# Converting 64-bit weights between the matmuls of eight experts: smaller pieces with two buffers, and an output layer that goes row block by row block

## The chip, the cores and the metric

The kernel runs on 1 core of a Trainium2 chip. The metric is the device time of one execution in microseconds; a version is given by the median of its runs.

## What is computed

Three layers follow each other. A recurrent attention (an mLSTM: 2 batches, 8 heads, 768 steps, head size 40) gives 1536 tokens of 320 numbers. A mixture of 8 experts sends each token to two of them. A last layer multiplies, applies a softmax-weighted unit and a normalisation, and multiplies again. Cut to what matters here:

```python
for e in range(E):                       # 8 experts, 320 -> 1024 -> 320
    for k in range(2):
        mask = top2[:, k] == e
        h = np.maximum(x[mask] @ w1[e], 0.0)
        out[mask] += top2_w[mask, k, None] * (h @ w2[e])
...
h = x @ w_in                             # the last layer
...
ln = (solu - mu) / np.sqrt(var + 1e-06) * g_ln
return ln @ w_out
```

The weights `moe2_w_in` and `moe2_w_out` of the last layer arrive as 64-bit floats. The kernel turns them into 32-bit floats on the chip, with integer operations on the two halves of each number.

## The kernel before

All matrix products are made from high and low parts: an operand is split into a part that TensorE multiplies as it is and the rest, and two or three products are added. So each weight is first split, on ScalarE (`split_hi`, line 117, a copy that rounds) and on VectorE or GpSimd (`split_lo`, line 121, the difference).

The expert stage is the loop over e at line 1019. The experts' row counts fall (`CAPS`: 448, 448, 432, 416, 404, 396, 384, 448); of expert 0 the first 192 rows are done before the loop. For each expert:

- The hidden layer, called L1 here. Eight groups f of 128 hidden columns: `layer1` (lines 127 to 134) makes 8 matmuls into an accumulator `ph`; `cut_h` then writes the hidden values, first the rounded part on ScalarE (line 139), then the rest on VectorE (line 140, and line 142 for the last 64 rows). The accumulators rotate: groups 0, 1, 3 to 7 share two, group 2 has one of another pool, so group 3 needs the accumulator of group 0. Between the groups stand three splits of the next expert's first weights (low parts on GpSimd, 128x1024 each), the transposes that prepare the next expert's rows (`prep_x`, line 988), and the load of the rows of the expert after that.
- The output layer, called L2 here. `layer2` (lines 149 to 154) makes, for one group f and one block n of 128 rows, 3 matmuls into the accumulator `pos[n]` (2 for a last short block of 64 rows). The loop is over f outside and n inside, so all row blocks end together. After each f stands one step of the conversion, and after every second f one split of the next expert's second weights (`split`, line 1025: ScalarE, VectorE, and a new load into the buffer that came free).
- `put(n)` (line 1055): the accumulator is copied to `YS`, on VectorE (line 164) except for n = 2, which goes on ScalarE; a short block is an addition on VectorE behind a copy on ScalarE (lines 161 and 162). GpSimd scatters the rows to DRAM (line 166).

The conversion (`convert`, line 928) takes a piece of raw weights `R` that SyncE has loaded, and makes one ScalarE instruction (line 937, a square that finds tiny numbers) and seven on VectorE (lines 938 to 942, 946, 947); the result in `u` is stored to DRAM (line 948), from where it is loaded as the weights of a ninth "expert". There are six pieces, five of 1024 columns and one of 512, in the order `cvs`: first `wout`, then `win`. The tiles `R`, `u`, `sc` and `sq` have one buffer each. The seven VectorE steps run through all experts as one sequence, one step after each f of experts 1 to 6; the next raw piece is loaded when the fifth instruction has read the old one.

```python
            act.activation(sq, hi.bitcast(F32), AF.Square)
            yield ve.tensor_scalar(u, hi, 3, (1 << 30) - 1, op0=ALU.logical_shift_left, op1=ALU.bitwise_and)
...
            sp.dma_start(dst[:, c0 : c0 + n], uf)
```

The order of instructions on each engine is that of the program text: no scheduler moves them, and an engine that waits holds everything behind it.

Expert 7 is written apart (line 1084): its L2 already goes row block by row block, and the tiles of the last layer's first steps take over the memory of the conversion's tiles by their tags.

Of the kernel before, what the change touches and what calls it, by code (L numbers as in the profile page):

```python
# [8 lines left out]
F32 = mybir.dt.float32  # L9
F32R = mybir.dt.float32r  # L10
BF16 = mybir.dt.bfloat16
I32 = mybir.dt.int32
# [8 lines left out]
DM, NE, DFF, NT = 320, 8, 1024, 1536  # L21
P = 128
# [14 lines left out]
def fused_kernel(ctx: ExitStack, tc, qt, kt, kv, og, ig, fg, wgn, noise, w1, w2, win, wout, gln, cst, out):  # L37
# [12 lines left out]
    wi32 = dp.tile([P, 3 * DFF], F32, name="wi32")  # L50
# [857 lines left out]
    with ExitStack() as pbx:  # L908
# [5 lines left out]
        psh = pbx.enter_context(tc.tile_pool(name="psh", bufs=2, space=PSUM))  # L914
        pso = pbx.enter_context(tc.tile_pool(name="pso", bufs=1, space=PSUM))

        cvs = (3, 4, 5, 0, 1, 2)
        raw = {}

        def load_raw(i):  # L920

            src = win if i < 3 else wout
            c0 = (i % 3) * DFF
            n = min(DFF, src.shape[1] - c0)
            R = raw[i] = b1.tile([P, DFF, 2], I32, tag="R", name=f"cvR{i}")[:, :n]
            sp.dma_start(R.rearrange("p n t -> p (n t)"), src[:, c0 : c0 + n].bitcast(I32))

        def convert(i):

            R, dst = raw[i], (wi32 if i < 3 else wo32)  # L930
            c0, n = (i % 3) * DFF, R.shape[1]
            u = b1.tile([P, DFF], I32, tag="u", name=f"cvu{i}")[:, :n]
            sc = b1.tile([P, DFF], I32, tag="sc", name=f"cvs{i}")[:, :n]
            sq = b1.tile([P, DFF], F32, tag="sq", name=f"cvq{i}")[:, :n]
            lo, hi = R[:, :, 0], R[:, :, 1]
            uf, scf = u.bitcast(F32), sc.bitcast(F32)
            act.activation(sq, hi.bitcast(F32), AF.Square)  # L937
            yield ve.tensor_scalar(u, hi, 3, (1 << 30) - 1, op0=ALU.logical_shift_left, op1=ALU.bitwise_and)
            yield ve.scalar_tensor_tensor(u, hi, -(1 << 30), u, op0=ALU.bitwise_and, op1=ALU.bitwise_or)
            yield ve.tensor_scalar(sc, u, -(1 << 23), None, op0=ALU.bitwise_and)  # L940
            yield ve.scalar_tensor_tensor(lo, lo, 9, sc, op0=ALU.logical_shift_right, op1=ALU.bitwise_or)
            ve.tensor_sub(scf, lo.bitcast(F32), scf)
            if i != cvs[-1]:
                load_raw(cvs[cvs.index(i) + 1])
            yield
            yield ve.scalar_tensor_tensor(uf, scf, 2.0**-20, uf, op0=ALU.mult, op1=ALU.add)
            ve.scalar_tensor_tensor(uf, sq, 2.0**-30, uf, op0=ALU.is_ge, op1=ALU.mult)
            sp.dma_start(dst[:, c0 : c0 + n], uf)
            yield

        X = {}
# [42 lines left out]
                act.activation(v["H"][0:64, d, 0:r], pt[0:64, 0:r], AF.Copy)  # L994
                ve.tensor_sub(v["H"][64:128, d, 0:r], pt[64:128, 0:r], v["T"][64:128, 0:r].bitcast(F32))

        def conversions():
            for i in cvs:
                yield from convert(i)

        X[0] = dict(x=rest, n=CAP - EARLY, w=[P] * ((CAP - EARLY) // P))
        load_x(1)

# [11 lines left out]
                    prep_x(0, d)  # L1015
        for n in range(2):
            put_y((0, n), YS[n], early["po"][n], T3, eti[:, n : n + 1], n == 1, ve)
        cv = conversions()
        for e in range(NE):
            n_e = X[e]["n"]  # L1020
            XH, XL = (X[e][k][:, :, 0:n_e] for k in "HL")
            new_w(e + 1, wsp1 if e % 2 == 0 else wsp0)
            hs = []

            def split(j):
                split_hi(e + 1, j)
                split_lo(e + 1, j, pool if j < 3 and e + 1 < NE else ve)
                if e + 2 < NE or e + 2 == NE and j != 2:
                    load_w(e + 2, j)

            for f in range(8):
                ph = (pst if f == 2 else psh).tile([P, CAP], F32, tag="pt" if f == 2 else "ph", name=f"ph{e}_{f}")[:, 0:n_e]
                layer1(ph, splits[e], XH, XL, f)
                h = bh.tile([P, 2 * CAP], F32R, tag="h", name=f"h{e}_{f}")
                cut_h(h, ph, n_e)
                hs.append(h)
                if e + 1 == NE and f % 2 == 0:
                    gain(NE, 3 + f // 2)
                if f % 2 and f < 7:
                    split(f // 2 + (3 if e + 1 == NE else 0))  # L1040
                if e == 0 and f == 7:
                    load_raw(cvs[0])
                if e + 1 < NE:
                    if f == 1:
                        alloc_x(e + 1)
                    if f in (2, 4, 6):
                        prep_x(e + 1, f // 2 - 1)
                    if f == 6 and e + 2 < NE:
                        load_x(e + 2)
            ws = X[e]["w"]  # L1050
            pos = [pos_tile(n, f"po{e}_{n}") for n in range(len(ws))]
            YS = [b1.tile([P, DM], F32, tag=f"YS{n}", name=f"YS{e}_{n}") for n in range(len(ws))]
            T3 = b1.tile([P, DM], F32, tag="T3", name=f"T3{e}")

            def put(n):
                put_y((e, n, 1), YS[n], pos[n], T3, X[e]["ti"][:, n : n + 1], ws[n] < P, act if n == 2 and e + 1 < NE else ve)

            if e + 1 < NE:
                for f in range(8):
                    for n in range(len(ws)):  # L1060
                        layer2(pos[n], splits[e], hs[f], f, n, n_e)
                    if e > 0:
                        next(cv, None)
                    if f % 2 == 0:
                        split(3 + f // 2)
                for n in range(len(ws)):
                    put(n)
                if e == NE - 2:
                    load_w(NE, 2)
            else:  # L1070
                tags = dict(Y="R", x2="u", XH="sc", XL="sq", T="T", pt="pt")
                held = {}

                def newb(t):
                    def new(k, shape, dt):
                        if k not in ("Y", "x2"):
                            return (pst if k == "pt" else b1).tile(shape, dt, tag=tags[k], name=f"c{k}{t}")
                        if k not in held:
                            held[k] = b1.tile([P, 3 if k == "Y" else 2] + shape[1:], dt, tag=tags[k], name=f"c{k}")
                        return held[k][:, t]  # L1080

                    return new

                for n in range(4):
                    for f in range(8):
                        layer2(pos[n], splits[e], hs[f], f, n, n_e)
                        if n == 0 and f == 0:
                            split(6)
                        if n == 1 and f < 3:
                            split(f)  # L1090
                        if n == 3 and f == 4:
                            xt(0, newb(0))
                            split_x(0, newb(0))
                    put(n)
                    if n < 3:
                        ahead.append((n, load_y(n, newb(n))))
                    if n == 2:
                        mix(0, newb(0))
                mix(1, newb(1))
# [202 lines left out]
```

## Time and profile before

| | us |
|---|---|
| median of 3 runs | 458.82 |
| lowest and highest run | 456.35, 461.11 |
| profiled execution, its time | 459.58 |
| its span in the trace | 457.5 |
| TensorE busy | 433.5 (95% of the span) |
| VectorE busy | 297.1 (65%) |
| ScalarE busy | 238.9 (52%) |
| GpSimd busy | 191.8 (42%) |

The span is the trace's own length; the execution takes 2.1 us more around it. Line numbers are those of the kernel before. PE is TensorE (PEld its weight loads), DVE is VectorE, ACT ScalarE, POOL GpSimd, SP SyncE; an engine's name with q is its queue.

### The profile page before, as it was taken

How to read it: one execution, taken by the hardware profiler on the slowest of the kernel's cores; microseconds unless marked ns; L12 is line 12 of the kernel's file. 1: busy time of each engine (PE TensorE's matmuls, PEld its weight loads, DVE VectorE, ACT ScalarE, POOL GpSimd, SP SyncE). 2: the span in 40 equal slices, each digit the busy share in tenths (PEclk: the TensorE clock that was granted, in tenths of full speed). 3: DMA queues.
4: the chain of work that ended last, by engine and by line, in shares of the span. 5: the costliest groups of instructions: out<-in, count | busy, mean ns of one | idle time of the engine just before them, and what ended most of it. 6: DMA issues, size and time to landing. Idle time of an engine off the chain costs nothing.

```text
span 457.5 us, 8125 instructions
## 1 busy us (share of the span) xinstructions
PE 433.5 (95%) x2777; PEld 407.1 (89%) x2777; DVE 297.1 (65%) x722; ACT 238.9 (52%) x517; POOL 191.8 (42%) x277
## 2 busy tenths in 40 slices
PE   7998979999989999999999969979999999999996
PEld 4887979998978989899999969969999789989996
DVE  8696698797446558575647665486355877556541
ACT  4687574661327362644626156236382776665542
POOL 8534666676317250541807218045203253342340
PEclk9999785896599999999999998989999999999999
DMA  6777894664424947375483834834602411120001
GB/s 187 245 225 219 295 273 133 229 239 148 179 85 143 323 135 271 125 239 181 129 302 91 319 113 137 295 101 127 211 1 102 147 45 43 45 85 16 29 16 43
DMA packets 36094, 71.73 MB, mean 157 GB/s; under 512 B 4225, under 2 KB 18981, under 8 KB 35408
## 3 DMA queue, kind: packets, MB, share of 16 engines
q1 hardware_dynamic: 32896, 62.06, 42.3%
q0 software_dynamic: 2912, 8.68, 5.2%
q8 instruction: 24, 0.39, 0.4%
q10 hardware_dynamic: 240, 0.41, 0.3%
q14 instruction: 22, 0.18, 0.1%
HBM read 55.50 MB, written 16.21 MB: 157 GB/s over the span
## 4 chain that ended last, share of the span: by engine, by line
PE 51%; DVE 9%; DMA 5%; issue 3%; ACT 1%; DVEq 0%; ACTq 0%
PE cpo L1173 3%; PE cpo L1175 3%; PE cpo L1174 3%; PE ph L127 3%; DMA wi<-cvu 3%; PE po L149 3%; PE po L150 3%; PE po L151 3%; PE pz L1165 2%; PE ph L128 2%; PE ph L133 2%; PE ph L130 2%; PE ph L132 2%; PE ph L129 2%; PE ph L131 2%
## 5 line engine op out<-in xcount | busy, mean ns | idle before, releaser
L166 POOL DMA_INDIRECT yt<-YS,ti x29 | 28.9, 995 | 126.4 <-DVE YS L164 119.8
L140 DVE SCALAR_TENSOR_TENSOR h<-ph,h 128x384 fp32r<-128x384 f32 (+1 forms) x64 | 34.3, 537 | 39.6 <-ACT h L139 39.5
L121 POOL TENSOR_TENSOR w0l<-r,w0h 128x1024 fp32r<-128x1024 f32 x23 | 54.7, 2408 | 9.8 <-ACT w0h L117 9.5
L139 ACT ACTIVATE h<-ph 128x448 fp32r<-128x448 f32 (+6 forms) x64 | 32.0, 503 | 48.1 <-PE ph L134 47.5
L149 PE MATMUL po<-w1h,h 128*128 128x320 f32 x184 | 56.8, 308 | 0.0
L151 PE MATMUL po<-w1h,h 128*128 128x320 f32 x184 | 56.7, 308 | 0.0
L150 PE MATMUL po<-w1l,h 128*128 128x320 f32 x184 | 56.7, 308 | 0.0
L476 POOL DMA_INDIRECT xg<-x,slots x24 | 25.8, 1075 | 27.6 <-DVE ix L444 12.5
L149 PEld LDWEIGHTS po<-w1h,h 128*128 128x128 f32 x184 | 34.6, 188 | 0.0
L150 PEld LDWEIGHTS po<-w1l,h 128*128 128x128 f32 x184 | 34.6, 188 | 0.0
L151 PEld LDWEIGHTS po<-w1h,h 128*128 128x128 f32 x184 | 34.6, 188 | 0.0
L340 PE MATMUL S<-Qb,Kb 128*128 128x128 f32 x192 | 32.9, 310 | 0.0
L127 PE MATMUL ph<-XH,w0h 128*128 128x448 f32 (+6 forms) x64 | 24.5, 383 | 7.9 <-DVE h L142 4.8
L121 DVE TENSOR_TENSOR w1l<-r,w1h 128x640 fp32r<-128x640 f32 x34 | 31.3, 934 | 0.4 <-ACT w1h L117 0.4
L937 ACT ACTIVATE cvq<-cvR 128x1024 f32<-128x1024 f32 (+1 forms) x6 | 6.3, 1052 | 46.0 <-DMA cvR<-in_win_dram 27.2
L1167 DVE TENSOR_TENSOR ZL<-pz,ZH 128x512 fp32r<-128x512 f32 x24 | 15.4, 685 | 22.6 <-ACT ZH L1166 22.6
L1173 PE MATMUL cpo<-w1h,ZH 128*128 128x320 f32 x96 | 30.0, 312 | 0.0
L1175 PE MATMUL cpo<-w1h,ZL 128*128 128x320 f32 x96 | 29.7, 309 | 0.0
L1174 PE MATMUL cpo<-w1l,ZH 128*128 128x320 f32 x96 | 29.7, 309 | 0.0
L117 ACT ACTIVATE w0h<-r 128x1024 fp32r<-128x1024 f32 x27 | 28.2, 1051 | 0.0
L340 PEld LDWEIGHTS S<-Qb,Kb 128*128 128x128 f32 x192 | 27.6, 214 | 0.1
L380 PE MATMUL Y<-KV,E 128*128 128x41 f32 x192 | 27.0, 296 | 0.0
(266 smaller groups left out, 1262.2 us busy)
## 6 DMA issues: line engine op xcount, KB each, us to landing
r<-in_w_dram SPq DMA_DIRECT2D x24, 512.0 KB
r<-in_w_dram SPq DMA_DIRECT2D x32, 320.0 KB
E<-gd SPq DMA_DIRECT2D x8, 512.0 KB
X<-xg SPq DMA_DIRECT2D x7, 579.0 KB
KV<-in_kv_dram SPq DMA_DIRECT2D x12, 324.0 KB
cY<-yt SPq DMA_DIRECT2D x12, 320.0 KB
cvR<-in_win_dram SPq DMA_DIRECT2D x3, 1024.0 KB
cvR<-in_wout_dram SPq DMA_DIRECT2D x2, 1024.0 KB
```

The costliest lines, as they stand in the source:

```text
L121: eng.tensor_sub(splits[e][2 * m + 1][:, k : k + n], raws[e, j], splits[e][2 * m][:, k : k + n].bitcast(F32))
L127: pe.matmul(ph, W1H[:, 0, fs], XH[:, 0], start=True, stop=False)
L139: act.activation(h[:, 0:n], ph, AF.Relu)
L140: ve.scalar_tensor_tensor(h[:, n + r : n + r + w], ph[:, 0:w], 0.0, h[:, 0:w].bitcast(F32), op0=ALU.max, op1=ALU.subtract)
L149: pe.matmul(po, hh, W2H[:, f], start=a, stop=False)
L150: pe.matmul(po, hh, W2L[:, f], start=False, stop=False)
L151: pe.matmul(po, hl, W2H[:, f], start=False, stop=z)
L166: i = pool.indirect_dma_start(out=yt, out_offset=bass.IndirectOffsetOnAxis(ap=idx[0:w], axis=0), in_=YS[0:w], in_offset=None, bounds_check ...
L340: pe.matmul(S[:, a], Kb[i % 3][j][:, a], Qb[i % 3][:, a], start=True, stop=True)
L1173: pe.matmul(po, ZH[:, f], W2H[:, f], start=(f == 0), stop=False)
L1174: pe.matmul(po, ZH[:, f], W2L[:, f], start=False, stop=False)
L1175: pe.matmul(po, ZL[:, f], W2H[:, f], start=False, stop=(f == 7))
```

## The change

A piece has 512 columns: five pieces of `wout` and six of `win`, eleven in all, in that order. `R`, `u` and `sq` have two buffers each, by the piece's parity; `sc` keeps one. Experts 1 to 5 convert two pieces each and expert 6 one; a piece's load is issued when the piece two before it has been read. The L2 of experts 0 to 6 goes row block by row block; a step is one group f of one block, a conversion step follows two of three steps, and the splits stand after steps 0, 6, 12 and 18 (0, 3, 6 and 9 in expert 0). `put(n)` follows its row block, and its copy is on ScalarE for every n except in expert 7. The tiles of the last layer's start take other tags.

```diff
-        cvs = (3, 4, 5, 0, 1, 2)
+        CW = 512
+        cvs = [(wo32, wout, c) for c in range(0, 8 * DM, CW)] + [(wi32, win, c) for c in range(0, 3 * DFF, CW)]
...
         def load_raw(i):
 
-            src = win if i < 3 else wout
-            c0 = (i % 3) * DFF
-            n = min(DFF, src.shape[1] - c0)
-            R = raw[i] = b1.tile([P, DFF, 2], I32, tag="R", name=f"cvR{i}")[:, :n]
-            sp.dma_start(R.rearrange("p n t -> p (n t)"), src[:, c0 : c0 + n].bitcast(I32))
+            if i < len(cvs):
+                _, src, c = cvs[i]
+                R = raw[i] = b1.tile([P, CW, 2], I32, tag=f"R{i % 2}", name=f"cvR{i}")
+                sp.dma_start(R.rearrange("p n t -> p (n t)"), src[:, c : c + CW].bitcast(I32))
...
-            u = b1.tile([P, DFF], I32, tag="u", name=f"cvu{i}")[:, :n]
-            sc = b1.tile([P, DFF], I32, tag="sc", name=f"cvs{i}")[:, :n]
-            sq = b1.tile([P, DFF], F32, tag="sq", name=f"cvq{i}")[:, :n]
+            R, (dst, _, c) = raw[i], cvs[i]
+            u = b1.tile([P, CW], I32, tag=f"u{i % 2}", name=f"cvu{i}")
+            sc = b1.tile([P, CW], I32, tag="sc", name=f"cvs{i}")
+            sq = b1.tile([P, CW], F32, tag=f"sq{i % 2}", name=f"cvq{i}")
...
-            if i != cvs[-1]:
-                load_raw(cvs[cvs.index(i) + 1])
+            load_raw(i + 2)
...
-            sp.dma_start(dst[:, c0 : c0 + n], uf)
+            sp.dma_start(dst[:, c : c + CW], uf)
...
                 if e == 0 and f == 7:
-                    load_raw(cvs[0])
+                    load_raw(0)
+                    load_raw(1)
...
-                put_y((e, n, 1), YS[n], pos[n], T3, X[e]["ti"][:, n : n + 1], ws[n] < P, act if n == 2 and e + 1 < NE else ve)
+                put_y((e, n, 1), YS[n], pos[n], T3, X[e]["ti"][:, n : n + 1], ws[n] < P, act if e + 1 < NE else ve)
 
             if e + 1 < NE:
-                for f in range(8):
-                    for n in range(len(ws)):
+                cv = chain(*(convert(i) for i in range(2 * e - 2, min(2 * e, len(cvs))) if e > 0))
+                for n in range(len(ws)):
+                    for f in range(8):
                         layer2(pos[n], splits[e], hs[f], f, n, n_e)
-                    if e > 0:
-                        next(cv, None)
-                    if f % 2 == 0:
-                        split(3 + f // 2)
-                for n in range(len(ws)):
+                        s = 8 * n + f
+                        if s % 3 < 2:
+                            next(cv, None)
+                        q = 6 if e > 0 else 3
+                        if s % q == 0 and s < 4 * q:
+                            split(3 + s // q)
                     put(n)
...
-                tags = dict(Y="R", x2="u", XH="sc", XL="sq", T="T", pt="pt")
...
+                tags = dict(Y=("R0", "R1", "Y2"), x2=("u0", "u1"), XH=("sq0",), XL=("sq1",), T=("T",), pt=("pt", "pt"))
```

VectorE at the end of the L2 of expert 4 and the start of the L1 of expert 5, before. `cv` marks the conversion's tiles with the piece's number (here pieces of `win`), `w1l_5` the low parts of expert 5's second weights, `YS4_n` the copies of expert 4's row blocks, `h5_0` the first hidden group of expert 5.

```order
L947 SCALAR_TENSOR_TENSOR cvu0_4191<-cvq0_4193,cvu0_4191 128x1024
L938 TENSOR_SCALAR cvu1_4475<-cvR1_4433 128x1024
L121 TENSOR_TENSOR w1l_5_4248<-r5_5_4178,w1h_5_4247 128x640
L939 SCALAR_TENSOR_TENSOR cvu1_4475<-cvR1_4433,cvu1_4475 128x1024
L940 TENSOR_SCALAR cvs1_4476<-cvu1_4475 128x1024
L121 TENSOR_TENSOR w1l_5_4248<-r5_6_4210,w1h_5_4247 128x640
L941 SCALAR_TENSOR_TENSOR cvR1_4433<-cvR1_4433,cvs1_4476 128x1024
L164 COPY YS4_0_4400<-po4_0_4396 128x320
L164 COPY YS4_1_4401<-po4_1_4397 128x320
L162 TENSOR_TENSOR YS4_3_4403<-po4_3_4399,T34_4404 64x320
L140 SCALAR_TENSOR_TENSOR h5_0_4558<-ph5_0_4549,h5_0_4558 128x384
```

The same place after the change; lines behind the conversion's first have moved by one to three.

```order
L945 SCALAR_TENSOR_TENSOR cvu6_4445<-cvq6_4447,cvu6_4445 128x512
L937 TENSOR_SCALAR cvu7_4502<-cvR7_4225 128x512
L938 SCALAR_TENSOR_TENSOR cvu7_4502<-cvR7_4225,cvu7_4502 128x512
L121 TENSOR_TENSOR w1l_5_4285<-r5_5_4203,w1h_5_4284 128x640
L939 TENSOR_SCALAR cvs7_4503<-cvu7_4502 128x512
L940 SCALAR_TENSOR_TENSOR cvR7_4225<-cvR7_4225,cvs7_4503 128x512
L941 TENSOR_TENSOR cvs7_4503<-cvR7_4225,cvs7_4503 128x512
L944 SCALAR_TENSOR_TENSOR cvu7_4502<-cvs7_4503,cvu7_4502 128x512
L121 TENSOR_TENSOR w1l_5_4285<-r5_6_4236,w1h_5_4284 128x640
L945 SCALAR_TENSOR_TENSOR cvu7_4502<-cvq7_4504,cvu7_4502 128x512
L162 TENSOR_TENSOR YS4_3_4440<-po4_3_4436,T34_4441 64x320
L140 SCALAR_TENSOR_TENSOR h5_0_4608<-ph5_0_4599,h5_0_4608 128x384
```

Before, a piece begins in the middle of the sequence and its tail stands behind the hidden groups of the next expert; now two whole pieces lie within one L2, piece 7 has another `u` than piece 6, and the two copies are gone from this engine.

ScalarE at the same place, from the last hidden group of expert 4 to the first of expert 5, before. `w1h_5` are the high parts of the weights, `cvq` the square.

```order
L139 ACTIVATE h4_7_4392<-ph4_7_4383 128x404
L117 ACTIVATE w1h_5_4247<-r5_3_4119 128x640
L117 ACTIVATE w1h_5_4247<-r5_4_4149 128x640
L937 ACTIVATE cvq1_4477<-cvR1_4433 128x1024
L117 ACTIVATE w1h_5_4247<-r5_5_4178 128x640
L117 ACTIVATE w1h_5_4247<-r5_6_4210 128x640
L164 ACTIVATE YS4_2_4402<-po4_2_4398 128x320
L161 ACTIVATE T34_4404<-po4_3_4399 64x320
L139 ACTIVATE h5_0_4558<-ph5_0_4549 128x396
```

The same after the change.

```order
L139 ACTIVATE h4_7_4429<-ph4_7_4420 128x404
L936 ACTIVATE cvq6_4447<-cvR6_4163 128x512
L117 ACTIVATE w1h_5_4284<-r5_3_4139 128x640
L117 ACTIVATE w1h_5_4284<-r5_4_4167 128x640
L164 ACTIVATE YS4_0_4437<-po4_0_4433 128x320
L936 ACTIVATE cvq7_4504<-cvR7_4225 128x512
L117 ACTIVATE w1h_5_4284<-r5_5_4203 128x640
L164 ACTIVATE YS4_1_4438<-po4_1_4434 128x320
L117 ACTIVATE w1h_5_4284<-r5_6_4236 128x640
L164 ACTIVATE YS4_2_4439<-po4_2_4435 128x320
L161 ACTIVATE T34_4441<-po4_3_4436 64x320
L139 ACTIVATE h5_0_4608<-ph5_0_4599 128x396
```

The copies of `YS` now stand between the squares and splits, each behind its row block, and there are two squares instead of one.

## Rows read from the trace of the kernel before

**Rows 1.** Waits, experts 1 to 6: engine, line, waited for; us, times, longest.

```profile
DVE cvu L938 <- DMA wo<-cvu: 14.7, 3, 6.1
DVE cvu L938 <- DMA wi<-cvu: 12.6, 2, 6.6
PE ph L127 <- DVE h L142: 4.8, 3, 3.9
PE ph L127 <- DVE h L140: 3.1, 1, 3.1
```

**Rows 2.** Stretches: length, busy PE PEld DVE ACT POOL, PEclk, DMA share, GB/s.

```profile
154.60:169.87 15.27, 15.27 (x79) 13.37 (x77) 7.33 (x22) 8.76 (x14) 9.05 (x6) 1.00 0.64 226
169.87:182.77 12.90, 12.90 (x89) 12.90 (x88) 11.01 (x14) 4.07 (x6) 0.18 (x2) 1.00 0.74 241
182.77:198.01 15.24, 14.75 (x78) 13.37 (x77) 8.23 (x24) 10.48 (x17) 9.92 (x10) 1.00 0.39 137
...
210.89:225.51 14.62, 14.23 (x78) 13.30 (x77) 9.18 (x26) 9.40 (x17) 9.61 (x10) 1.00 0.33 103
...
238.36:252.43 14.07, 13.99 (x78) 13.12 (x77) 10.62 (x27) 9.36 (x17) 9.42 (x10) 1.00 0.31 98
...
265.36:283.60 18.24, 14.35 (x76) 14.00 (x74) 11.92 (x26) 10.66 (x19) 10.11 (x10) 0.91 0.32 96
...
296.45:314.47 18.02, 14.93 (x79) 14.04 (x77) 12.57 (x22) 9.14 (x16) 10.43 (x10) 0.91 0.34 99
...
338.27:351.20 12.93, 12.93 (x90) 12.92 (x89) 6.89 (x11) 4.95 (x7) 3.92 (x6) 1.00 0.22 73
```

**Rows 3.** Two stretches within the L1 of expert 5.

```profile
270.20:274.06 3.86, 0.00 (x0) 0.03 (x1) 3.86 (x9) 0.62 (x2) 1.08 (x2) 1.00 0.46 128
274.06:277.50 3.44, 3.44 (x11) 3.43 (x12) 1.75 (x7) 0.64 (x2) 2.94 (x5) 0.55 0.40 144
```

**Rows 4.** VectorE in time: start, us, engine, line; in brackets idle before, releaser.

```profile
258.37 0.82 DVE L121 TENSOR_TENSOR w1l<-r,w1h 128x640 fp32r<-128x640 f32 x1
259.11 1.22 DVE L947 SCALAR_TENSOR_TENSOR cvu<-cvq,cvu 128x1024 f32<-128x1024 f32 x1
266.97 0.69 DVE L938 TENSOR_SCALAR cvu<-cvR 128x1024 int32<-128x1024 int32 x1 [6.64 <-DMA wi<-cvu]
...
273.24 0.54 DVE L140 SCALAR_TENSOR_TENSOR h<-ph,h 128x384 fp32r<-128x384 f32 x1
```

**Rows 5.** VectorE's groups by line and form: busy us, mean ns of one.

```profile
L164 DVE COPY YS<-po 128x320 f32<-128x320 f32 x17 | 7.7, 484 | 9.9 <-PE po L151 9.9
...
L942 DVE TENSOR_TENSOR cvs<-cvR,cvs 128x512 f32<-128x512 f32 x1 | 0.7, 693 | 0.0
...
L940 DVE TENSOR_SCALAR cvs<-cvu 128x512 int32<-128x512 int32 x1 | 0.5, 468 | 0.0
L938 DVE TENSOR_SCALAR cvu<-cvR 128x512 int32<-128x512 int32 x1 | 0.4, 427 | 4.6 <-DMA wo<-cvu 4.6
```

**Rows 6.** SyncE in time: the raw piece used in the L2 of expert 4.

```profile
257.22 0.34 SPq L926 DMA_DIRECT2D cvR<-in_win_dram  x1
```

**Rows 7.** ScalarE in time, end of expert 4's L2, and one group.

```profile
264.91 1.13 ACT L937 ACTIVATE cvq<-cvR 128x1024 f32<-128x1024 f32 x1 [10.46 <-DMA cvR<-in_win_dram]
265.94 1.35 ACT L117 ACTIVATE w1h<-r 128x640 fp32r<-128x640 f32 x2
...
L164 ACT ACTIVATE YS<-po 128x320 f32<-128x320 f32 x6 | 2.6, 429 | 7.6 <-issue 7.5
```

**Rows 8.** GpSimd and VectorE in time, experts 4 and 5.

```profile
251.79 2.44 POOL L121 TENSOR_TENSOR w0l<-r,w0h 128x1024 fp32r<-128x1024 f32 x1
253.84 1.49 DVE L941 SCALAR_TENSOR_TENSOR cvR<-cvR,cvs 128x1024 int32<-128x1024 int32 x1
...
274.11 0.97 POOL L166 DMA_INDIRECT yt<-YS,ti  x1 [0.22 <-DVE h L142]
```

**Rows 9.** VectorE: the cut of expert 5's eighth group, L2 from 283.60.

```profile
285.14 0.21 DVE L142 SCALAR_TENSOR_TENSOR h<-ph,h 128x64 fp32r<-128x64 f32 x1
```

More of the change, by code (lines that the diff above doesn't have):

```diff
@@ L915, in fused_kernel @@
         pso = pbx.enter_context(tc.tile_pool(name="pso", bufs=1, space=PSUM))
-        cvs = (3, 4, 5, 0, 1, 2)
+        CW = 512
+        cvs = [(wo32, wout, c) for c in range(0, 8 * DM, CW)] + [(wi32, win, c) for c in range(0, 3 * DFF, CW)]
         raw = {}
         def load_raw(i):
-            src = win if i < 3 else wout
-            c0 = (i % 3) * DFF
-            n = min(DFF, src.shape[1] - c0)
-            R = raw[i] = b1.tile([P, DFF, 2], I32, tag="R", name=f"cvR{i}")[:, :n]
-            sp.dma_start(R.rearrange("p n t -> p (n t)"), src[:, c0 : c0 + n].bitcast(I32))
-        def convert(i):
-            R, dst = raw[i], (wi32 if i < 3 else wo32)
-            c0, n = (i % 3) * DFF, R.shape[1]
-            u = b1.tile([P, DFF], I32, tag="u", name=f"cvu{i}")[:, :n]
-            sc = b1.tile([P, DFF], I32, tag="sc", name=f"cvs{i}")[:, :n]
-            sq = b1.tile([P, DFF], F32, tag="sq", name=f"cvq{i}")[:, :n]
+            if i < len(cvs):
+                _, src, c = cvs[i]
+                R = raw[i] = b1.tile([P, CW, 2], I32, tag=f"R{i % 2}", name=f"cvR{i}")
+                sp.dma_start(R.rearrange("p n t -> p (n t)"), src[:, c : c + CW].bitcast(I32))
+        def convert(i):
+            R, (dst, _, c) = raw[i], cvs[i]
+            u = b1.tile([P, CW], I32, tag=f"u{i % 2}", name=f"cvu{i}")
+            sc = b1.tile([P, CW], I32, tag="sc", name=f"cvs{i}")
+            sq = b1.tile([P, CW], F32, tag=f"sq{i % 2}", name=f"cvq{i}")
             lo, hi = R[:, :, 0], R[:, :, 1]
@@ L995, in prep_x @@
                 ve.tensor_sub(v["H"][64:128, d, 0:r], pt[64:128, 0:r], v["T"][64:128, 0:r].bitcast(F32))
-        def conversions():
-            for i in cvs:
-                yield from convert(i)
         X[0] = dict(x=rest, n=CAP - EARLY, w=[P] * ((CAP - EARLY) // P))
@@ L1017, in fused_kernel @@
             put_y((0, n), YS[n], early["po"][n], T3, eti[:, n : n + 1], n == 1, ve)
-        cv = conversions()
         for e in range(NE):
@@ L1070, in fused_kernel @@
             else:
-                tags = dict(Y="R", x2="u", XH="sc", XL="sq", T="T", pt="pt")
-                held = {}
+                tags = dict(Y=("R0", "R1", "Y2"), x2=("u0", "u1"), XH=("sq0",), XL=("sq1",), T=("T",), pt=("pt", "pt"))
                 def newb(t):
[L1075 to L1082, printed above, removed]
+                    return lambda k, shape, dt: (pst if k == "pt" else b1).tile(shape, dt, tag=tags[k][t], name=f"c{k}{t}")
                 for n in range(4):
```

## The prediction

> **What bounds the kernel now.** I read the idle times of TensorE first, then the stretch in which they lie, then the queue of the engine that ended them. In the list of waits for the experts' stretch [rows 1] the reader is to see that TensorE waits there for one thing only: the first matmul of a hidden-layer group (line 127) for a VectorE instruction of an earlier group (lines 140 and 142, the second half of `cut_h`), 4.8 + 3.1 us. The same list has a longer wait on another engine: VectorE stands 14.7 + 12.6 us at line 938, the first instruction of a conversion, for the store of the conversion before.
>
> The table of stretches [rows 2] gives the hidden layer (L1) and the output layer (L2) of each expert. An L2 takes 12.9 us whoever is late. The L1s are uneven: 15.27 us for expert 1 with 448 rows and 14.07 for expert 4 with 404 are full to within 0.1 us, so a row costs (15.27 - 14.07)/44 = 0.0273 us. By that line expert 2 (432 rows) should take 14.83, expert 3 (416) 14.40, expert 5 (396) 13.85 and expert 6 (384) 13.52; they take 15.24, 14.62, 18.24 and 18.02. The excess is 0.41 + 0.22 + 4.39 + 4.50 = 9.52 us, more than the 7.9 us of idle time. The rest is clock: in expert 5 TensorE stands still for 3.86 us, and the 3.44 us behind that are granted 0.55 of full speed on the mean, mostly the lower of its two levels, 1.2 of 2.4 GHz [rows 3].
>
> VectorE's queue says why [rows 4]. The last instruction of one conversion ends at 260.33 us and the next conversion, first in line behind it, has one buffer `u` with it; it starts at 266.97, when the store has landed, 6.64 us later. Behind it in the queue stand three conversion instructions, two weight splits, two copies of `YS` and one addition; only at 273.24 comes the cut of the first hidden group of expert 5, whose L1 began at 265.36 [rows 2]. TensorE needs that group's accumulator for its fourth group at 270.2. So a DMA round trip, through VectorE's order, stops TensorE. ScalarE is held in the same way: the load of a raw piece is issued at 257.22 [rows 6], in the middle of the L2 that uses it, and line 937 begins at 264.91 after 10.46 us [rows 7], with two splits and the copies behind it.
>
> **The change part by part.** *Two buffers.* Pieces alternate between `R0`/`R1`, `u0`/`u1`, `sq0`/`sq1`, and piece i uses what piece i - 2 used, one expert earlier. A store then has one expert's L1 plus L2 (27 us) to land instead of none; the one shown took about 6.6 [rows 4]. A load is issued when piece i - 2 is half done, some 20 us before its use; the one shown took 264.91 - 257.22 = 7.7 us [rows 6, 7]. Halved transfers need not take half: between nothing saved (7.7 and 6.6) and half, both ends are far below 20, so I put both waits at zero. This takes all of the 9.52 us, if VectorE isn't late for another reason.
>
> *Smaller pieces, more instructions.* A 1024-column piece costs VectorE 5 x 1.22 + 2 x 0.69 = 7.5 us [rows 4]; a 512-column piece 0.43 and 0.47 plus, at 0.69 for each of the five with two inputs, 3.45: 4.35 us [rows 5]. Eleven pieces are 47.9 us where five whole ones and a half took 41.9: 6.0 us more. Against it 14 copies of `YS`, of 0.48 us each [rows 5], go from VectorE to ScalarE: 6.8 us less. For VectorE the two cancel.
>
> *Does VectorE finish inside an L2?* In experts 1 to 5 there are two pieces, 8.7 us, and four splits of 0.82 [rows 4], 3.28. The cut of the eighth group ends 1.75 us after the L2 of expert 5 began (285.14 + 0.21 - 283.60) [rows 9], and the first split waits, as I estimate, some 0.5 us for ScalarE's half of it. Sum 14.2, less some 0.07 that neighbours overlap, 18 times: about 13 us, when L2 ends at 12.9. Then comes one addition, 0.47 us, and the first cut. TensorE misses that cut only at its fourth group, 270.20 - 265.36 = 4.84 us into L1 [rows 2, 3]: at 17.7, so with 0.7 for the cut and 0.5 for the addition VectorE may run until 16.5. There are 3.5 us to spare, five times. I put the cost at zero. Below zero it can't go, since all the stall is counted already; above, the bound is that every halved instruction keeps the whole price, which is rival C.
>
> *Copies on ScalarE.* Three copies of 0.43 us, two squares of at most 1.13 each and four splits of 0.68 (two took 1.35) are 6.3 us of 12.9 [rows 7]. The copies stand in its queue where TensorE finishes each row block, with squares and splits between; ScalarE waits there for TensorE, never the other way, since the accumulators are wanted again an expert later. GpSimd's scatters now start during L2 instead of behind it (the second one shown began at 274.11 [rows 8]); TensorE has no wait for them in the list [rows 1].
>
> *Row block by row block.* The same matmuls in another order. Expert 7 already goes this way and takes 12.93 us for what expert 1 does in 12.90 [rows 2]: zero. But the eighth hidden group is now wanted after 21 matmuls (12.9/88 each: 3.1 us) instead of 77 (11.3 us). Its cut is done at 1.75: 1.3 us to spare. Zero again, with a price if the cut slips by more.
>
> *Weight splits* move forward, to steps 0, 6, 12, 18 of 32 where they stood at 0, 8, 16, 24; their loads were issued an expert earlier. Nothing. Expert 0 converts nothing; only its two copies change engine.
>
> *Tail.* The last piece is stored earlier in expert 6's L2, and the tiles of the final stage take other tags; TensorE runs that stretch without a wait on them. Zero.
>
> The sum: the profiled execution takes 459.58 us; 459.58 - 9.5 = 450.1. The median of the runs is 458.82, 0.76 lower, so I forecast 449.3.
>
> **The rivals.** *A, part of the stall stays.* GpSimd's scatters now run while VectorE converts. The trace has one conversion instruction beside a GpSimd subtraction, 1.49 us instead of 1.22 [rows 8], 0.27 more. With 0.27 on all 14, VectorE runs until 16.8, at the edge of 16.5; half a microsecond more puts it 0.8 late in five L1s: 4 us, 453.3. Against: a scatter, 0.97 us [rows 8], is much shorter than that subtraction, 2.44, and three in an L2 meet only some of the 14.
> The Trainium skill, page "SBUF — State Buffer", section "Who interferes with whom", says that a VectorE instruction with two SBUF inputs contends with a GpSimd instruction that reads SBUF, and that the later one waits for the other to finish. That speaks against this change: ten of the fourteen have two such inputs. The row with 1.49 us agrees in kind. If three scatters held VectorE for their full 0.97 us, it would run until 15.9, still in time. The rule therefore adds chance to A and takes nothing from the sum.
>
> *B, no change.* The waits move from stores to loads: a raw piece or a split's weights arrive late at ScalarE, which now also holds every copy, and VectorE waits behind it. Expert 1's L2 shows a DMA share of 0.74 [rows 2], so a queue can be long. The time would be that of before, 458 to 459. Against: a load needs 7.7 us and has 20.
>
> *C, slower.* The place is VectorE's queue at the end of L2 of experts 1 to 5. If halved instructions cost what whole ones do (two inputs 1.22, one input 0.69), two pieces take 15.0 instead of 8.7 and VectorE runs until 19.3, 2.8 past 16.5. Each of five L1s then loses some 3 us and, as in experts 5 and 6, some clock behind it (4.39 - 3.86 = 0.5 and, with the wait of 3.1 in rows 1, 4.50 - 3.1 = 1.4): 4 us each, 20 us against the forecast: 469. It costs anything from 3.5 us of growth on, and outweighs the gain when the growth passes 3.5 + 9.5/5 = 5.4 us. The 512-column piece that the trace has [rows 5] speaks against it.
>
> **How the numbers follow.** The forecast has 0.80, A 0.09, B 0.06, C 0.05. A measurement of this kernel tells about 1% from no change, so "faster" is below 454.2: the forecast and half of A and a little more, 0.85; "same" is B and the rest of A, 0.09; "slower" C and a tail, 0.06. The range: the forecast, with the spread of the runs of before (0.5% either way, 2.5 us) below, 446.8, and just past A's 453.3 above, 453.6.
>
> **What would show it right or wrong.** Right: no wait of VectorE at the first conversion instruction for a store, none of ScalarE for a raw piece, L1s of 14.8, 14.4, 14.1, 13.9 and 13.5 us for experts 2 to 6 with a granted clock of 1.00, L2s still 12.9, and scatters spread over L2. Wrong: VectorE busy past the end of L2 by over 3 us, or idle time of TensorE inside an L2 at the first row block's last step (line 149 or 151 waiting for line 140 or 142), or ScalarE idle before line 936.

## The result and the profile after

The changed kernel takes 446.94 us (median of 4 runs, 446.12 to 448.29); the kernel before, on the same chip, 459.13. The ratio is 0.9742 with a 95% interval of 0.9685 to 0.9798: faster by 2.6%. The profiled execution takes 448.29 us, its span is 446.4; before it was 459.58 and 457.5, so 11.3 us are gone, where the prediction said 9.5. The forecast was 449.3; 446.94 lies only 0.14 us above the lower end of its range, 446.8, and two of the four runs lie below that end.

The table of stretches of the kernel after, the L1s of experts 1 to 6, among them the L2 of expert 4, and at last everything from the L1 of expert 1 to the start of the L2 of expert 7 (length, busy time of PE, PEld, DVE, ACT, POOL, granted clock, DMA share, GB/s):

```profile
154.89:170.16 15.27, 15.27 (x79) 13.37 (x77) 6.64 (x20) 9.20 (x15) 7.97 (x4) 1.00 0.63 225
183.06:197.83 14.77, 14.77 (x79) 13.38 (x77) 7.19 (x22) 8.96 (x15) 7.78 (x4) 1.00 0.47 150
210.70:224.91 14.21, 14.21 (x78) 13.31 (x77) 7.20 (x22) 8.86 (x15) 7.66 (x4) 1.00 0.49 154
237.73:251.65 13.92, 13.92 (x78) 13.10 (x77) 7.20 (x22) 8.79 (x15) 7.59 (x4) 1.00 0.50 156
251.65:264.48 12.83, 12.83 (x89) 12.83 (x89) 11.80 (x21) 5.46 (x10) 4.44 (x8) 1.00 0.80 262
264.48:277.15 12.67, 12.67 (x76) 12.55 (x74) 6.60 (x19) 8.53 (x15) 7.20 (x4) 1.00 0.51 157
290.00:303.29 13.29, 13.29 (x79) 12.47 (x78) 6.28 (x14) 8.72 (x15) 7.46 (x4) 1.00 0.45 138
...
154.89:327.08 172.19, 172.19 (x1032) 164.78 (x1031) 115.69 (x244) 94.58 (x167) 71.47 (x66) 1.00 0.61 196
```

Beside [rows 2]: in every stretch TensorE's busy time is now the stretch itself, and the clock is 1.00 in all of them, where the L1s of experts 5 and 6 had 0.91. The same stretch of before is 183.67 us with 175.73 busy and a clock of 0.98. So 11.48 us are gone there: 7.94 of idle time, and 3.54 of busy time for the same 1032 matmuls. This stretch, from expert 1's first hidden matmul to expert 7's first output matmul, is what I compare below: it doesn't carry the attention stage, which ends between 151.6 and 155.6 us in the profiles; medians that differ by less than those 4 us are therefore judged by the stretch.

The list of waits of experts 1 to 6 (154.89 to 313.84 us), cut to the engines that answer to [rows 1]. No line has TensorE waiting for `cut_h`, none has VectorE waiting for a store or ScalarE for a raw piece; ScalarE waits for TensorE, as its copies now stand behind each row block:

```profile
DVE h L140 <- ACT h L139: 42.7, 48, 3.8
ACT h L139 <- PE ph L134: 25.9, 25, 1.3
ACT T L161 <- PE po L154: 9.3, 5, 1.9
```

VectorE in time in the L2 of expert 4, which begins at 251.65 and ends at 264.48, beside [rows 4]. Each row gives start, us, engine, line, and in brackets the idle time before and its releaser:

```profile
252.91 0.21 DVE L142 SCALAR_TENSOR_TENSOR h<-ph,h 128x64 fp32r<-128x64 f32 x1
...
258.95 0.42 DVE L937 TENSOR_SCALAR cvu<-cvR 128x512 int32<-128x512 int32 x1
259.41 0.69 DVE L938 SCALAR_TENSOR_TENSOR cvu<-cvR,cvu 128x512 int32<-128x512 int32 x1
...
264.03 0.68 DVE L945 SCALAR_TENSOR_TENSOR cvu<-cvq,cvu 128x512 f32<-128x512 f32 x1
...
266.73 0.56 DVE L140 SCALAR_TENSOR_TENSOR h<-ph,h 128x384 fp32r<-128x384 f32 x1 [1.09 <-ACT h L139]
```

The second piece begins at 258.95 with nothing in brackets: no store is waited for. The last conversion instruction ends at 264.71, 13.06 us after the L2 began; the prediction's sum was "about 13". The first cut of expert 5 now waits for ScalarE's half of the same group (1.09 us), where before that result waited for VectorE.

### The profile page after: what moved, and what is told of

Same layout as the page of the kernel before. It is cut to its first block, busy times and chain, and to the rows that moved or that the text cites. A ratio compares the mean times of both kernels' runs of the same rounds, so it can differ in the third digit from the quotient of the medians.

```text
span 446.4 us, 8210 instructions
## 1 busy us (share of the span) xinstructions
PE 430.3 (96%) x2777; PEld 404.0 (91%) x2777; DVE 298.7 (67%) x743; ACT 245.7 (55%) x536; POOL 196.5 (44%) x277
## 4 chain that ended last, share of the span: by engine, by line
PE 68%; DVE 0%; ACT 0%; issue 0%; DVEq 0%; ACTq 0%
PE po L150 6%; PE po L151 6%; PE po L149 6%; PE ph L127 3%; PE cpo L1161 3%; PE cpo L1163 3%; PE cpo L1162 3%; PE ph L128 3%; PE ph L133 3%; PE ph L132 3%; PE ph L134 3%; PE ph L130 3%; PE ph L129 3%; PE ph L131 3%; PE pt L986 2%; PE pz L1153 2%
## 5 line engine op out<-in xcount | busy, mean ns | idle before, releaser
L166 POOL DMA_INDIRECT yt<-YS,ti x29 | 31.8, 1097 | 85.8 <-ACT YS L164 55.4
L164 ACT ACTIVATE YS<-po 128x320 f32<-128x320 f32 x20 | 8.8, 439 | 37.2 <-issue 31.1
L380 PEld LDWEIGHTS Y<-KV,E 128*128 128x128 f32 x192 | 26.7, 215 | 0.1
```

The costliest lines, as they stand in the source:

```text
L166: i = pool.indirect_dma_start(out=yt, out_offset=bass.IndirectOffsetOnAxis(ap=idx[0:w], axis=0), in_=YS[0:w], in_offset=None, bounds_check ...
L380: pe.matmul(T[i]["Y"][:, h], T[i]["E"][:, h], values(i)[:, h], start=(c == 0 and h == 0), stop=(h == NH - 1))
```

## The experiments

The theory on trial (theory 1) is the prediction's: a DMA round trip in VectorE's queue, from a buffer that the next conversion needs at once, makes the first cut of the next expert late. Theory 2 is the rival that lies in the same diff: the order by row blocks and the copies that left VectorE bring the gain. Each run is compared by its median and by the stretch from expert 1's L1 to expert 7's L2; idle is the stretch's length less TensorE's busy time. The runs were made on several chips; the ratio compares each with runs of the kernel before on the same one.

| run | median us | ratio to before (95%) | stretch us | idle us |
|---|---|---|---|---|
| before | 459.13 | | 183.67 | 7.94 |
| after | 446.94 | 0.9742 (0.9685 to 0.9798) | 172.19 | 0.00 |
| `pieces_only` | 446.52 | 0.9700 (0.9659 to 0.9741) | 172.41 | 0.00 |
| `order_only` | 461.21 | 1.0079 (1.0034 to 1.0124) | 187.77 | 11.52 |
| `one_u` | 455.55 | 0.9912 (0.9885 to 0.9939) | 180.15 | 6.36 |
| `one_R` | 451.53 | 0.9821 (0.9779 to 0.9864) | 176.05 | 2.90 |
| `u_two` | 455.11 | 0.9859 (0.9780 to 0.9938) | 179.66 | 4.76 |
| `extra4` | 446.72 | 0.9695 (0.9627 to 0.9764) | 172.17 | 0.00 |
| `extra8` | 462.87 | 1.0066 (1.0030 to 1.0103) | 188.91 | 12.51 |
| `late7_rows` | 449.97 | 0.9803 (0.9743 to 0.9864) | 175.88 | 2.32 |
| `late7_groups` | 450.66 | 0.9821 (0.9757 to 0.9885) | 174.56 | 1.82 |
| `full_t` | 441.21 | 0.9589 (0.9516 to 0.9661) | 167.51 | 0.00 |
| `best` | 443.71 | 0.9647 (0.9589 to 0.9704) | 167.86 | 0.00 |

### The conversion alone, and the order alone

`pieces_only` keeps the new conversion and takes the old L2 back:

```diff
-                for n in range(len(ws)):
-                    for f in range(8):
+                for f in range(8):
+                    for n in range(len(ws)):
                         layer2(pos[n], splits[e], hs[f], f, n, n_e)
...
+                    for _ in range(2):
+                        next(cv, None)
+                    if f % 2 == 0:
+                        split(3 + f // 2)
+                for n in range(len(ws)):
                     put(n)
```

(and the copies of row blocks 0 and 1 go back to VectorE.)

> The changed kernel with only the conversion changed: pieces of 512 with two buffers, but L2 with the row blocks inside the loop over groups and the copies on VectorE as before. Theory 1: nearly the whole gain, 446 to 450, with VectorE 0.9 us later at the end of L2, inside its spare 3.5 us. Theory 2: 456 to 460.

`order_only` is the kernel before with the new L2:

```diff
-                for f in range(8):
-                    for n in range(len(ws)):
+                for n in range(len(ws)):
+                    for f in range(8):
                         layer2(pos[n], splits[e], hs[f], f, n, n_e)
-                    if e > 0:
-                        next(cv, None)
...
+                        if e > 0 and s % len(ws) == 0:
+                            next(cv, None)
...
-                for n in range(len(ws)):
                     put(n)
```

(with the splits' steps and the copies on ScalarE as in the changed kernel.)

> The kernel before with only the order of L2 changed: row block by row block, copies on ScalarE, splits at the new steps; conversion in pieces of 1024 columns with one buffer. Theory 1: VectorE waits for stores as before, only 0.9 us of copies are gone from behind the wait, so 455 to 459. Theory 2: most of the gain, 447 to 450.

Measured: 446.52 and 461.21. The conversion alone has the whole gain (stretch 172.41 against 172.19), so theory 2 falls; the order and the copies alone make the kernel a little slower, which neither theory expected. The waits for raw pieces on ScalarE in the kernel before, then the waits of `order_only` in the expert stage:

```profile
ACT cvq L937 <- DMA cvR<-in_win_dram: 27.2, 3, 10.5
ACT cvq L937 <- DMA cvR<-in_wout_dram: 18.8, 2, 9.5
```

```profile
DVE cvu L938 <- DMA wo<-cvu: 16.4, 3, 7.2
ACT cvq L937 <- DMA cvR<-in_win_dram: 14.0, 3, 6.4
DVE cvu L938 <- DMA wi<-cvu: 13.9, 2, 7.2
ACT cvq L937 <- DMA cvR<-in_wout_dram: 5.8, 2, 5.4
PE ph L127 <- DVE h L142: 4.1, 4, 3.0
PE ph L127 <- DVE h L140: 3.3, 1, 3.3
PE ph L127 <- ACT XH L990: 2.7, 1, 2.7
```

VectorE still waits for stores, 16.4 + 13.9 us instead of 14.7 + 12.6, and TensorE has the old two waits and a third of 2.7 us, in the L1 of expert 2. ScalarE's own waits for raw pieces fell, from 27.2 + 18.8 to 14.0 + 5.8 us, so they aren't what made it slower. Why the stores landed later there was not tried.

### One buffer back at a time

`one_u` and `one_R` are the changed kernel with one buffer for the result, and one for the raw piece (whose load must then be issued one piece ahead, not two):

```diff
-            u = b1.tile([P, CW], I32, tag=f"u{i % 2}", name=f"cvu{i}")
+            u = b1.tile([P, CW], I32, tag="u0", name=f"cvu{i}")
```

> The changed kernel with one buffer for the result u instead of two; all else stays. Theory 1 (the store's round trip, waited for in VectorE's queue, was what stopped TensorE): in experts 1 to 5 the second piece's first instruction waits some 5 to 6 us for the store of the first, VectorE runs until about 19 us after the start of L2, 2.5 past the 16.5 at which TensorE misses the cut, and five hidden layers lose 3 to 4 us each: 458 to 466. Theory 2 (the gain came from the order of the row blocks and the copies that left VectorE): 447 to 449.

```diff
-                R = raw[i] = b1.tile([P, CW, 2], I32, tag=f"R{i % 2}", name=f"cvR{i}")
+                R = raw[i] = b1.tile([P, CW, 2], I32, tag="R0", name=f"cvR{i}")
...
-            load_raw(i + 2)
+            load_raw(i + 1)
```

> The changed kernel with one buffer for the raw piece R: a load is issued when the piece before it has been read. Theory 1 in its wider form (load and store are each long enough to hold the queue when they have one buffer): the second piece's load is issued 5 us into L2 and takes 5 to 8, so ScalarE and VectorE wait until 11 to 13, VectorE runs until about 18, 1.5 past the limit: 453 to 458. Theory 2: 447 to 449.

Measured 455.55 and 451.53: both slower than the changed kernel, both a little under the range for theory 1 (by 2.5 and 1.5 us). VectorE of `one_u` in time, at the end of the L2 of expert 4 that began at 255.29 and in the L1 behind it, and GpSimd beside the last row:

```profile
261.98 0.69 DVE L945 SCALAR_TENSOR_TENSOR cvu<-cvq,cvu 128x512 f32<-128x512 f32 x1
266.60 0.43 DVE L937 TENSOR_SCALAR cvu<-cvR 128x512 int32<-128x512 int32 x1 [3.92 <-DMA wi<-cvu]
...
271.66 0.69 DVE L945 SCALAR_TENSOR_TENSOR cvu<-cvq,cvu 128x512 f32<-128x512 f32 x1
...
273.85 2.52 DVE L183 SCALAR_TENSOR_TENSOR ti<-X,tf 128x3 int32<-128x3 f32 x1
```

```profile
273.94 2.40 POOL L121 TENSOR_TENSOR w0l<-r,w0h 128x1024 fp32r<-128x1024 f32 x1
```

The store of a 512-column piece holds VectorE for 3.92 us, not the 5 to 6 that I had put in, so VectorE runs until 272.35, 17.06 us after the L2 began: 0.6 past the limit of 16.5, and TensorE's wait there is 0.55. Two more waits of 0.48 and 0.54 follow in the same L1 (it takes 14.81 us instead of 12.67). They stand behind line 183, an instruction of three columns that takes 0.21 us in the changed kernel: here it meets a weight split on GpSimd and ends with it, at 276.3. The late VectorE brings this about: its addition ends at 272.74, GpSimd's last scatter starts at 273.01 and the first split at 273.94. The same is seen in the L1s of experts 2 to 6. In sum 4.4 of the 6.36 us of idle time come behind line 183, and only some 2.0 at or before the fourth group.

The waits of `one_R` at the conversion's first instruction:

```profile
DVE cvu L937 <- DMA cvR<-in_wout_dram: 4.6, 2, 2.8
DVE cvu L937 <- DMA wi<-cvu: 3.5, 1, 3.5
DVE cvu L937 <- DMA cvR<-in_win_dram: 3.4, 1, 3.4
```

The instruction is held up to 3.5 us. Most of the time goes to the load by name; the row that names a store is not that of a buffer which the instruction needs, since `u` has two. So the raw piece is the second cause, and by the stretch (3.9 us against 8.0 in `one_u`) the smaller one.

`u_two` goes the other way: the kernel before, with a second result buffer only (and the square in 16 bits, to make room).

```diff
-            u = b1.tile([P, DFF], I32, tag="u", name=f"cvu{i}")[:, :n]
+            u = b1.tile([P, DFF], I32, tag=f"u{cvs.index(i) % 2}", name=f"cvu{i}")[:, :n]
...
-            sq = b1.tile([P, DFF], F32, tag="sq", name=f"cvq{i}")[:, :n]
+            sq = b1.tile([P, DFF], BF16, tag="sq", name=f"cvq{i}")[:, :n]
```

> The kernel before with a second buffer for the result u alone, pieces of 1024 columns and everything else as it was (the square is kept in 16 bits to make room). The store is no longer waited for; the raw piece still has one buffer. Theory 1 in its wider form: VectorE's first conversion instruction then waits for the load, which in the profile of before arrived about 2 us earlier than the store, so some 2 us of each 6 go: 451 to 456, and the wait reads DMA cvR instead of DMA wo or wi. A rival (the store alone was the cause): 446 to 449.

Measured 455.11, inside the range for theory 1. Its waits at the same instruction:

```profile
DVE cvu L938 <- DMA cvR<-in_win_dram: 11.1, 3, 5.3
PE ph L127 <- DVE h L140: 3.4, 1, 3.4
DVE cvu L938 <- DMA cvR<-in_wout_dram: 3.1, 2, 1.6
PE ph L127 <- DVE h L142: 1.3, 1, 1.3
```

The 27.3 us for the stores have become 14.2 us for the loads: the load had stood behind the store all the time, and one buffer alone buys 4.0 of the 11.5 us that the stretch lost. The whole gain needs both buffers. `one_R` has that one second buffer too, but pieces of half the size (and the new L2, worth nothing in `pieces_only`), and gains 7.6 of the 11.5: this speaks for the smaller pieces as a part of the gain. No run has whole pieces with both buffers, so how much of it is theirs stays open.

### How much room VectorE has

`extra4` and `extra8` put four or eight instructions of 0.71 us at the end of the conversion in experts 1 to 5:

```diff
                         if s % 3 < 2:
                             next(cv, None)
+                        if 1 <= e <= 5 and s >= 20 and s < 20 + 4:
+                            ve.scalar_tensor_tensor(xtra, xtra, 1.0, xtra, op0=ALU.mult, op1=ALU.mult)
```

> The changed kernel with four more VectorE instructions (512 columns, about 0.71 us each, on a tile of their own that nothing reads) at the end of the conversion in experts 1 to 5: VectorE runs until about 15.9 us after the start of L2, under the 16.5 of the prediction. No change from the changed kernel: 446 to 448.5. If the spare time is smaller than worked out: 450 or more.

> The same with eight: VectorE runs until about 18.8, 2.3 past the limit. TensorE stands still at the fourth group of five hidden layers, with what follows in these layers and the clock 2 to 4 us each: 456 to 467. If VectorE's order has far more room than worked out: under 449.

Measured 446.72 and 462.87, both as expected. In `extra4` VectorE runs until 15.86 us after the L2 of expert 4 began (263.96 + 2.87 - 250.97), and TensorE is busy all through. VectorE of `extra8` at the same place, where the L2 began at 260.38, and TensorE's waits in that kernel:

```profile
273.37 5.77 DVE L1063 SCALAR_TENSOR_TENSOR xtra<-xtra 128x512 f32<-128x512 f32 x8
```

```profile
PE ph L127 <- DVE h L142: 8.3, 6, 2.2
PE ph L127 <- DVE h L140: 2.2, 2, 2.0
```

It runs until 279.14, 18.76 after the start, and TensorE stands still for 1.6 to 2.2 us at the fourth group of each of five L1s, where 18.76 - 16.5 = 2.3 was worked out. These are 9.6 of the 12.51 us of idle time; the rest comes behind line 183, which takes 2.5 to 2.8 us in these L1s beside GpSimd's split, as in `one_u`. The limit of 16.5 that was worked out from [rows 2, 3] lies between 15.86 (no wait) and 17.06 (0.55 us).

### How early the eighth hidden group is wanted

Four such instructions ahead of the cut of the eighth group, in the new order of L2 and in the old one:

```diff
+                if f == 7 and 1 <= e <= 6:
+                    for _ in range(4):
+                        ve.scalar_tensor_tensor(xtra, xtra, 1.0, xtra, op0=ALU.mult, op1=ALU.mult)
                 cut_h(h, ph, n_e)
```

> The changed kernel with four more VectorE instructions (0.71 us each, on a tile that nothing reads) ahead of the cut of the eighth hidden group in experts 1 to 6. Some 0.6 us of them fit into VectorE's idle time there, so the cut is done about 3.7 us after the start of L2 instead of 1.5. In the order row block by row block TensorE wants it after 3.1: a wait inside the first row block of six L2s, 0.6 us each and a little more: 449 to 453. If the order has more room: 446 to 448.5.

> The same four instructions in the kernel that has the new conversion and the old order of L2 (groups outside, row blocks inside), which wants the eighth group only after 11 us. No wait in L2; VectorE runs until about 16.5 at the end of L2, at the limit: 446 to 448.5. If the four instructions cost by themselves, whatever the order: as late7_rows.

Measured 449.97, as expected, and 450.66, a miss of 2 us, in the range of the rival that the four instructions cost by themselves. The two waits lie at different places. TensorE's weight loads in `late7_rows`, then TensorE's matmuls in `late7_groups`:

```profile
PEld po L151 <- DVE h L140: 3.9, 6, 1.1
```

```profile
PE ph L127 <- DVE h L140: 1.4, 1, 1.4
PE ph L127 <- DVE h L142: 0.4, 1, 0.4
```

By row blocks the wait is inside six L2s (line 151, the first product that takes the low part of the eighth group). In the changed kernel that product of expert 4 starts 3.35 us after the L2 began:

```profile
255.00 0.31 PE L151 MATMUL po<-w1h,h 128*128 128x320 f32 x1
```

The cut is done at 1.47, so the room is 1.9 us. In `late7_rows` it is done at 3.97 and the L2 takes 13.44 instead of 12.83 us; the six L2s are 0.4 to 1.1 us longer each. In the old order no L2 waits; there VectorE is past 16.5 (17.03 and 18.17) at the end of the L2s of experts 4 and 5, and the L1s of experts 5 and 6 pay. I had called that "at the limit" and given it nothing. What had been left out is GpSimd. VectorE's four added instructions in these two L2s, then GpSimd around the second, which began at 275.89:

```profile
249.77 3.86 DVE L1032 SCALAR_TENSOR_TENSOR xtra<-xtra 128x512 f32<-128x512 f32 x4
...
276.51 4.60 DVE L1032 SCALAR_TENSOR_TENSOR xtra<-xtra 128x512 f32<-128x512 f32 x4
```

```profile
271.22 7.15 POOL L121 TENSOR_TENSOR w0l<-r,w0h 128x1024 fp32r<-128x1024 f32 x3
```

Four such instructions take 2.87 us elsewhere (in `extra4`). Here the first of them meets the last of GpSimd's three splits, which ends at 278.37, and takes 2.42 us instead of 0.69. With 2.87 us for the four, VectorE would have ended at 16.0 and 16.4, under the limit. So by this sum the price in the old order comes from the place of the added instructions beside a split, not from the eighth group.

### The term that was too small

The prediction's line through the L1s gave expert 5 13.85 us; it takes 12.67. Expert 5 is the one that prepares rows without a short block (expert 6 has 384). `full_t` makes the short transposes from 128 rows:

```diff
+            if n % P:
+                pool.memset(v["x"][64:128, m], 0.0)
...
-                w, c = (P, n * P) if w == P else (64, r - 64)
-                pe.transpose(pt[:, c : c + w], v["x"][:w, n, d * P : (d + 1) * P], ident[:w, :w])
+                c = n * P if w == P else r - 64
+                pe.transpose(pt[:, c : c + P], v["x"][:, n, d * P : (d + 1) * P], ident)
```

> The changed kernel with the transposes of the short last row block of an expert made from 128 rows instead of 64 (the other 64 rows are set to zero by GpSimd, and what they give lies behind the columns that are read). Theory: the prediction's line through the hidden layers missed that expert 5 prepares rows without a short block; each short transpose costs TensorE some 0.35 us more than a full one, by its form, 18 times: 440 to 443. Rival (it is the wait for the second load of the rows, or simply a fourth transpose): 446 to 448.

Measured 441.21, as expected. TensorE's weight loads around the transposes in the L1 of expert 4, after and in `full_t`:

```profile
241.95 0.44 PEld L986 LDWEIGHTS pt<-consts,X 128*128 128x128 f32 x3
242.55 0.14 PEld L986 LDWEIGHTS pt<-consts,X 64*128 64x128 f32 x1 [0.17 <-DMA wi<-cvu]
242.75 0.19 PEld L127 LDWEIGHTS ph<-XH,w0h 128*128 128x128 f32 x1
```

```profile
237.19 0.55 PEld L988 LDWEIGHTS pt<-consts,X 128*128 128x128 f32 x4
237.71 0.19 PEld L127 LDWEIGHTS ph<-XH,w0h 128*128 128x128 f32 x1
```

With 64 rows the weight load stands off 0.17 us and the next one of 128 rows comes 0.20 us behind it: 242.75 - 241.95 = 0.80 us. With 128 rows it is 0.52. The store that the row names as releaser isn't the cause: other such rows name none, and all 15 waits of this kind in the stretch are gone in `full_t`. The L1s of experts 1 to 6 of `full_t`:

```profile
152.83:167.25 14.42, 14.42 (x79) 13.20 (x78) 6.39 (x20) 9.00 (x15) 7.72 (x4) 1.00 0.72 244
180.15:193.91 13.76, 13.76 (x79) 13.19 (x77) 6.89 (x22) 8.84 (x15) 7.47 (x4) 1.00 0.52 160
206.78:220.16 13.38, 13.38 (x79) 13.15 (x77) 6.94 (x22) 8.70 (x15) 7.40 (x4) 1.00 0.53 163
232.98:246.03 13.05, 13.05 (x78) 12.93 (x77) 6.92 (x22) 8.61 (x15) 7.32 (x4) 1.00 0.56 163
258.87:271.42 12.55, 12.55 (x75) 12.43 (x74) 6.60 (x19) 8.50 (x15) 7.21 (x4) 1.00 0.53 159
284.27:296.68 12.41, 12.41 (x79) 12.29 (x77) 5.92 (x13) 8.50 (x15) 7.19 (x4) 1.00 0.41 124
```

Five of the six are 0.83 to 1.01 us shorter, three short transposes each, 0.28 to 0.34 us for one. The fifth, which has none, is 0.12 shorter as well, so a little of the others' gain may not be the transposes'.

The Trainium skill, page "TensorEngine Tiling (Array Packing)", section "Key Properties", says that changing the tiling mode, not just the tile, drains TensorE. The rows agree in kind: the 0.17 and 0.20 us stand at the change of form in both directions, and they go when the form stays; whether it is a drain the profile doesn't show.

### Both together

`best` has the new conversion, the old L2 and the transposes of `full_t` (its diff is those two).

> The new conversion with the old order of L2 and the copies on VectorE, and the short transposes made from 128 rows. If order and copies add nothing to the conversion's two buffers: as full_t, 439 to 442. If they are worth something once TensorE is faster: 443 or more.

Measured 443.71, by the median in the range of "worth something once TensorE is faster". The trace doesn't bear that out: the stretch is 167.86 us against 167.51 in `full_t`, so in the experts the two are alike, and the profiled executions differ before them. Expert 1's L1 begins at 155.54 and 152.83, and the granted clock of the first 60 us is 0.92 and 0.97. `full_t`, the changed kernel with full transposes, has the lowest median, 441.21 us, 0.9589 of before; the intervals of the two overlap, so which is faster stays open.

## Why the prediction was right

- *The cause.* Right. The store's wait and the load's wait, through VectorE's order, made the cut late; with both buffers TensorE has no idle time in the stretch. `pieces_only` shows that the conversion is the whole of it, `one_u` and `u_two` that the store is one part and the load another that stands behind it. The smaller pieces, which the prediction counted as work that cancels, seem to be a part too.
- *Waits at zero.* Right: no wait for a store or a raw piece is left in the list. The halved store, where it is waited for (`one_u`), holds VectorE for 3.9 us; the whole one held it for 6.6 at the same place [rows 4].
- *VectorE ends at about 13 us, limit 16.5.* Right: 13.06, and the limit lies between 15.86 and 17.06. This was the place of rival C, and `extra8` is C in kind: 18.76 us, and 462.87.
- *Rival A, scatters beside the conversion.* It didn't come in the changed kernel. A two-input instruction of 512 columns takes 0.69 us there, as [rows 5] has it, but the scatters are longer, 1.10 us on the mean instead of 1.00 (before, then after):

```profile
L166 POOL DMA_INDIRECT yt<-YS,ti x29 | 28.9, 995 | 126.4 <-DVE YS L164 119.8
```

```profile
L166 POOL DMA_INDIRECT yt<-YS,ti x29 | 31.8, 1097 | 85.8 <-ACT YS L164 55.4 <-DVE YS L164 19.9 <-DVE YS L162 8.8
```

Its mechanism, VectorE held by GpSimd, is real all the same: in `one_u`, `extra8`, `order_only` and `late7_groups` single VectorE instructions of 0.2 or 0.7 us took 2.4 us and more beside GpSimd's splits, not its scatters.

- *Row blocks and copies at zero.* Right for time: 446.52 without them, 446.94 with them. The room was a little larger than worked out, 1.9 us and not 1.3: the prediction counted 21 matmuls up to the eighth group's first product, but VectorE's part is wanted only by the third, at 3.35 us. That passing it costs time is what `late7_rows` shows.
- *The sum.* The step that was off is the term "the excess is 0.41 + 0.22 + 4.39 + 4.50 = 9.52": it measured 0.47 + 0.41 + 0.15 + 5.57 + 4.73 = 11.33 us over experts 2 to 6. Its line went through two L1s that both contain short transposes; expert 5's has none, and 1.18 of the 1.81 us that were missed are there. The rest is small time in experts 3, 4 and 6: "full to within 0.1 us" had hidden 0.15 in expert 4. The profiled execution's own gain is 11.29 us, so the L1s account for it; the medians differ by 12.2, inside their spread. These 1.8 us are most of the 2.4 by which the forecast of 449.3 missed. That 446.94 still fell inside the range, by 0.14 us, is partly luck: its lower end was set by the spread of the runs alone and left nothing for an error of the sum.
- *Rival B.* It didn't come. `order_only` has the time that B names and a little more, but not by B's mechanism: ScalarE's waits for raw pieces fell there, and VectorE's waits for stores grew, with 11.52 us of idle time on TensorE.

## What to carry to other kernels

A DMA waited for on a busy in-order engine costs nothing there until the backlog behind it reaches an instruction that the bounding engine needs; work out that limit from the trace (here 16.5 us after the start of a layer) and compare the whole queue with it. Before giving one tile a second buffer, look for the next wait at the same instruction: here the load stood behind the store, and only both buffers gave the whole gain. When the time of a disturbed stretch is estimated from undisturbed ones, take those with the same instructions, and count the forms, not only the sizes. When an engine is made late, look also at what it now stands beside: in the slow variants VectorE's work moved onto GpSimd's splits, and a wait of half a microsecond became one and a half.

## What the runs showed of the hardware that I had not expected

A 64-row transpose between 128-row matmuls costs TensorE some 0.3 us more than one of 128 rows, although both take 0.27 us by their own row: the time is in the weight loads before and behind it. Making 18 of them full brought the stretch, which holds 15, from 172.19 to 167.51 us, and the median from 446.94 to 441.21. A halved store was waited for 3.9 us on VectorE (19.7 us in five waits of `one_u`) where the whole one took 5.5 on the mean (27.3 us in five [rows 1]): well over half. A VectorE instruction of three columns (line 183), 0.21 us by itself, took 2.5 us when a GpSimd split of 2.4 us started 0.09 us behind its start (`one_u`).
